# A load, attention work of two batches and one batch's phi moved in a fused linear attention and feed-forward kernel

## Chip, cores, metric

One core of one Trainium2 chip. The metric is device time of one execution in microseconds (us), the median of several.

## The reference, cut

```python
def phi(x):
    return np.where(x > 0, x, np.exp(x) - 1.0) + 1.0
# q, k, v: 8 batches, 8 heads, 576 positions, 64 per head
kv  = np.einsum('bhsd,bhse->bhde', phi(k), v)
z   = np.sum(phi(k), axis=2)
num = np.einsum('bhsd,bhde->bhse', phi(q), kv)
den = np.einsum('bhsd,bhd->bhs', phi(q), z)[..., None] + 1e-06
x   = (num / den)            # as 4608 tokens x 512
h   = x @ w_in               # 512 x 2048
out = (h - np.tanh(h)) @ w_out   # 2048 x 512
```

## The kernel before

The tokens go through the feed-forward part in nine chunks of 512. In a chunk, layer 1 makes 16 tiles of 128 hidden features (four matmuls each), a tanh on ScalarE (ACT) and a subtraction on VectorE (DVE) for two tiles at a time; layer 2 then has 16 slots of four matmuls. The attention of the next batches is sprinkled between: `s1[n]` is done behind tile n of layer 1, `s2[n]` behind slot n of layer 2.

```python
dense = Banks([0, 1, 2, 3, 4, 5])     # PSUM banks, in turn, for layers 1 and 2 from chunk 1 on
attn = Banks([6, 7])                  # for the attention of batches 2 and up

def l1act2(fi, h, gT):                # two tiles: their banks come free with the subtraction
    th = mpool.tile([128, 2, 512], F32, name="th")
    nc.scalar.activation(th, h, AF.Tanh)
    nc.vector.tensor_sub(gT[:, fi:fi + 2, :], h, th)                    # L373

# one half of phi of q or k: exp on ACT, then two instructions on DVE
(lambda: nc.scalar.activation(e, x, AF.Exp),                            # L134
 lambda: nc.vector.tensor_scalar(r, x, 0.0, 1.0, ALU.max, ALU.add),     # L135
 lambda: nc.vector.tensor_tensor(y, e, r, ALU.min))                     # L136

def a_spread(b):                      # 1/den to DRAM (ds) and back, spread over partitions (rdb)
    ds = dram.tile([H, 4, J * 16], F32, name="ds")
    for t in range(4):
        nc.sync.dma_start(out=ds[:, t, :], in_=rden_t[b][32 * t:32 * t + H, :])    # L305
    rdb = rpool.tile([128, NP, 4, J, 16], F32, name="rdb")
    for hh in range(2):
        nc.sync.dma_start(out=rdb[64 * hh:64 * hh + 64]...,                        # L308
                          in_=ds[4 * hh:4 * hh + 4]....partition_broadcast(64))
...
# the loads of a later batch wait until the transposing DMA of the next batch's q has landed
s1[0].append(lambda: (gate(qT_t[n1]), load_k(n2), load_q(n2), load_v(n2)))
...
elif n1 < B:                          # chunk 1: kv and den of batch 2 behind tiles 8 and 10
    s1[8 if c == 1 else 5].append(lambda: a_kv_cols(n1, attn))
    s1[10 if c == 1 else 8].append(lambda: (a_den(n1, attn), a_spread(n1)))
    for p in range(NP + 1):           # num, scaled by rdb, behind slots 12, 13, 14, 15, 15
        s2[min(12 + p, 15) if c == 1 else 9 + p].append(lambda p=p: a_num(n1, p))
```

`a_kv_cols` needs `vp`, a copy of v that VectorE makes (`a_vp`, L189). `a_num` puts a matmul (L317) into bank 6 or 7, which comes free when VectorE has multiplied by rdb (L328).

## Time and profile before

| | us |
|---|---|
| time, median of the 5 runs that go with the changed kernel's | 293.38 (293.09 to 293.61) |
| span of the profiled execution | 291.8 |
| TensorE busy | 285.5 (98%) |
| chunk 1: layer 1 starts, layer 2 starts | 50.24, 65.93 |
| chunk 2 starts | 80.72 |

The place where the change acts is 38 to 82 us. These are rows of TensorE's timeline there: start, length, engine and line, operation, result and operands, shapes, count, and in brackets the idle time just before and what ended it. A matmul's length is modelled and reaches into the next one's start: 512 columns show 0.379 us but start 0.216 apart, so read starts, and add 0.16 us to a bracketed idle time that follows such a matmul.

```profile
38.87 1.66 PE L177 MATMUL ps_all<-v,kp 64*128 64x192 bf16 x36 [0.22 <-DMA v<-in_v_dram]
...
50.24 8.07 PE L366 MATMUL ps_all<-xT,w_in_sb 128*128 128x512 bf16 x36
58.24 1.24 PE L199 MATMUL ps_all<-vp,kp 64*128 64x136 bf16 x36
...
65.93 11.39 PE L387 MATMUL ps_all<-w_out_sb,gT 128*128 128x512 bf16 x52
77.16 0.38 PE L317 MATMUL ps_all<-qT,kz 128*128 128x512 bf16 x1
...
79.31 0.38 PE L317 MATMUL ps_all<-qT,kz 128*128 128x512 bf16 x1
...
80.72 5.34 PE L366 MATMUL ps_all<-xT,w_in_sb 128*128 128x512 bf16 x24
```

The first row is kv of batch 1, with its wait for v. From 50.24 on come nine tiles (36 matmuls), kv of batch 2, the other seven tiles with den in between, layer 2, and the num matmuls between its last slots. None of these rows has a bracket; from the starts, TensorE loses some 0.2 us up to kv of batch 2 (36 x 0.216 from 50.24 is 58.0), 0.1 of it the gap that other narrow groups have ahead of them too, and nothing to speak of after.

### The profile page before, as it was taken

The numbers are of one execution on the slowest core, as the hardware profiler recorded it, in microseconds if no ns is written. First come the engines' busy times: TensorE is split into PE (matmuls) and PEld (weight loads), VectorE is DVE, ScalarE is ACT, GpSimd is POOL, SyncE is SP. The second block draws the span as 40 slices with busy tenths as digits, with TensorE's granted clock in tenths as the row PEclk, the third lists the DMA queues.
The fourth block names the chain that finished last, engine by engine and source line by source line (L and its number), as shares of the span: only waits on it lengthen the run. The fifth ranks groups of instructions, "written<-read, shape, count | busy, mean of one in ns | idle before, by whom it ended". The sixth has DMA issues, their size and how long they took to land.

```text
span 291.8 us, 4505 instructions
## 1 busy us (share of the span) xinstructions
PE 285.5 (98%) x1803; PEld 134.5 (46%) x1803; DVE 175.1 (60%) x266; ACT 139.7 (48%) x168; POOL 33.7 (12%) x56
## 2 busy tenths in 40 slices
PE   8999999999999999999999999999999999999994
PEld 3544464454454444444454444444544444444443
DVE  4759958987468674776478637865581457106600
ACT  4938548846354733465345534751551155126411
POOL 8674030110030003000300030000000000000000
PEclk9999999999999999999999999999999999999999
DMA  7999999997999768965895579666117310130032
GB/s 105 193 202 212 208 206 215 194 183 149 249 158 161 175 128 137 197 146 121 136 223 123 123 139 197 146 138 139 30 38 165 73 36 0 43 83 19 0 74 72
DMA packets 39093, 38.94 MB, mean 133 GB/s; under 512 B 16352, under 2 KB 33824, under 8 KB 38304
## 3 DMA queue, kind: packets, MB, share of 16 engines
q0 software_dynamic: 17568, 18.35, 39.0%
q1 hardware_dynamic: 21344, 20.17, 30.9%
q8 instruction: 14, 0.23, 0.3%
q10 hardware_dynamic: 160, 0.13, 0.1%
q14 instruction: 7, 0.06, 0.1%
HBM read 43.91 MB, written 9.55 MB: 183 GB/s over the span
## 4 chain that ended last, share of the span: by engine, by line
PE 85%; DMA 11%; POOL 2%; issue 1%; DVE 0%; POOLq 0%
PE ps_all L387 39%; PE ps_all L366 38%; DMA v<-in_v_dram 6%; DMA w_in_sb<-in_moe_w_in_dram 3%; PE ps_all L199 2%; DMA kraw<-in_k_dram 2%; PE ps_all L317 2%; PE ps_all L618 1%; PE ps_all L276 1%; POOL v L419 1%; PE ps_all L177 1%; POOL qraw L90 0%; PE ps_all L320 0%; POOL qraw L93 0%; POOL w_out_sb L115 0%
## 5 line engine op out<-in xcount | busy, mean ns | idle before, releaser
L366 PE MATMUL ps_all<-xT,w_in_sb 128*128 128x512 bf16 x574 | 127.6, 379 | 0.0
L387 PE MATMUL ps_all<-w_out_sb,gT 128*128 128x512 bf16 x560 | 127.5, 379 | 0.0
L373 DVE TENSOR_TENSOR gT<-ps_all,th 128x1024 bf16<-128x1024 f32 x64 | 77.9, 1218 | 59.2 <-ACT th L372 59.2
L372 ACT ACTIVATE th<-ps_all 128x1024 f32<-128x1024 f32 x64 | 65.6, 1025 | 57.1 <-PE ps_all L366 46.5
L366 PEld LDWEIGHTS <-w_in_sb 128*128 128x128 bf16 x574 | 55.0, 98 | 66.1 <-issue 0.3
L387 PEld LDWEIGHTS <-gT 128*128 128x128 bf16 x560 | 54.2, 98 | 64.2
L396 ACT COPY osb<-ps_all 128x512 f32<-128x512 f32 (+1 forms) x36 | 20.9, 583 | 71.8 <-PE ps_all L387 52.6
L328 DVE TENSOR_TENSOR xT<-ps_all,rdb 128x512 bf16<-128x512 f32 x24 | 16.5, 691 | 13.7 <-PE ps_all L317 11.2
L134 ACT ACTIVATE e<-qraw 128x1152 bf16<-128x1152 bf16 x16 | 18.5, 1160 | 8.2 <-DMA qraw<-in_q_dram 8.2
L134 ACT ACTIVATE e<-kraw 128x1152 bf16<-128x1152 bf16 x15 | 17.5, 1164 | 0.3 <-DMA kraw<-in_k_dram 0.3
L136 DVE TENSOR_TENSOR qp<-e,r 128x1152 bf16<-128x1152 bf16 x16 | 12.1, 758 | 8.0 <-ACT e L134 7.2
L136 DVE TENSOR_TENSOR kp<-e,r 128x1152 bf16<-128x1152 bf16 x15 | 11.4, 759 | 7.9 <-ACT e L134 6.9
L383 POOL COPY g<-qT 1x1 bf16<-1x1 bf16 x5 | 0.9, 178 | 119.2 <-DMA qT<-qp 119.2
L378 DVE TENSOR_TENSOR gT<-ps_all,th 128x512 bf16<-128x512 f32 x16 | 10.3, 686 | 2.4 <-ACT th L377 1.7
L377 ACT ACTIVATE th<-ps_all 128x512 f32<-128x512 f32 x16 | 9.2, 598 | 4.4 <-PE ps_all L366 3.2
L447 PE MATMUL ps_all<-zero 128*128 128x512 bf16 x29 | 9.2, 480 | 1.2 <-DVE zero L405 1.2
L317 PE MATMUL ps_all<-qT,kz 128*128 128x512 bf16 x28 | 10.1, 379 | 0.0
L135 DVE TENSOR_SCALAR r<-qraw 128x1152 bf16<-128x1152 bf16 x16 | 7.3, 454 | 2.1 <-DMA qraw<-in_q_dram 2.1
L199 PEld LDWEIGHTS <-kp 64*128 64x128 bf16 x216 | 6.4, 94 | 2.5 <-issue 2.1
L285 DVE RECIPROCAL rden<-den 128x144 f32<-128x144 f32 x7 | 7.4, 1053 | 0.2
L199 PE MATMUL ps_all<-vp,kp 64*128 64x136 bf16 x216 | 7.4, 220 | 0.0
L394 DVE COPY osb<-ps_all 128x128 f32<-128x128 f32 x1 | 0.3, 292 | 11.6 <-PE ps_all L618 11.6
(85 smaller groups left out, 123.6 us busy)
## 6 DMA issues: line engine op xcount, KB each, us to landing
out_dram<-osb SPq DMA_DIRECT2D x70, 128.0 KB
rdb<-ds SPq DMA_DIRECT2D x12, 576.0 KB
kraw<-in_k_dram POOLq DMA_DIRECT2D x7, 576.0 KB, 7.1
qraw<-in_q_dram POOLq DMA_DIRECT2D x7, 576.0 KB, 9.1
v<-in_v_dram POOLq DMA_DIRECT2D x7, 576.0 KB, 11.6
w_in_sb<-in_moe_w_in_dram POOLq DMA_DIRECT2D x6, 256.0 KB, 8.7
w_out_sb<-in_moe_w_out_dram POOLq DMA_DIRECT2D x3, 512.0 KB, 14.7
qraw<-in_q_dram POOLq DMA_DIRECT2D x2, 288.0 KB, 4.4
```

The source lines that it names most:

```text
L134: return (lambda: nc.scalar.activation(e, x, AF.Exp), lambda: nc.vector.tensor_scalar(r, x, 0.0, 1.0, ALU.max, ALU.add), lambda: nc.vector ...
L136: lambda: nc.vector.tensor_tensor(y, e, r, ALU.min))
L199: nc.tensor.matmul(ps[hg][:, i, :], kp[r, i, j].rearrange("p h d -> p (h d)"), vp[r, i, j, :], start=(j == 0), stop=(j == J - 1))
L317: nc.tensor.matmul(ps, kz[:, p // 2, p % 2, 0:128], qT[:, p % 2, 0:8, p // 2, :], start=True, stop=True)
L328: nc.vector.tensor_mul(xT[:, p, S * b:S * b + 512].rearrange("p (j t c) -> p j t c", j=8, t=4), ps.rearrange("p j (t c) -> p j t c", t=4), ...
L366: nc.tensor.matmul(h, w_in_sb[:, 2 * (p % 2) + p // 2, fi * 128:(fi + 1) * 128], xT[:, p, c * 512:(c + 1) * 512], start=(n == 0), stop=(n ...
L372: nc.scalar.activation(th, h, AF.Tanh)
L373: nc.vector.tensor_sub(gT[:, fi:fi + 2, :], h, th)
L377: nc.scalar.activation(th, h, AF.Tanh)
L378: nc.vector.tensor_sub(gT[:, fi, :], h, th)
L387: nc.tensor.matmul(o, gT[:, fi, i * 128:(i + 1) * 128], w_out_sb[:, fi, :], start=(fi == 0), stop=(fi == NF - 1))
L396: nc.scalar.copy(osb[:, f0:f1], o[:, f0:f1])
```

## The change

The intent, as the diff reads: TensorE stood idle for 0.4 us in chunk 0, waiting for v of batch 1. So kv of batch 1 goes two slots later (behind slot 9, with den and num behind slot 10), and half of a quarter of w_out, which slots 8 and 9, now ahead of kv, need, is loaded ahead of v. With attention of batch 1 later, phi of batch 2 moves later too: VectorE's part of k between the subtractions of chunk 1, v's copy, kv and den of batch 2 behind it. Chunk 1's first two tiles take pairs 0 and 1 of xT first.

```diff
-    load_v(1)
     for n in range(2):
+        if n == 1:
+            load_v(1)
         nc.gpsimd.dma_start(out=w_out_sb[:, 8 + 2 * n:10 + 2 * n, :], ...)
@@ chunk 0, behind slots of layer 2
-            s2[7].append(lambda: (a_qT_pe(1, 0, side), a_kv(1, side), a_qT_pe(1, 1, side)))
-            s2[8].append(lambda: b0_scale_rest(side))
-            s2[9].append(lambda: (a_den(1, side), num1(), a_split(1)))
-            s2[11].append(lambda: spread1(0))
+            s2[7].append(lambda: a_qT_pe(1, 0, side))
+            s2[8].append(lambda: a_qT_pe(1, 1, side))
+            s2[9].append(lambda: a_kv(1, side))
+            s2[10].append(lambda: (b0_scale_rest(side), a_den(1, side), num1(), a_split(1)))
+            s2[12].append(lambda: spread1(0))
-            s2[11].append(lambda: (exp2(qs, q_t, qp_t, "qp", 0), rest2(qs[0])))
+            s2[11].append(lambda: exp2(qs, q_t, qp_t, "qp", 0))
             s2[12].append(lambda: exp2(qs, q_t, qp_t, "qp", 1))
-            s2[13].append(lambda: (spread1(1), exp2(ks, k_t, kp_t, "kp", 0), rest2(qs[1]), a_qT_dma(2)))
-            s2[14].append(lambda: rest2(ks[0]))
+            s2[14].append(lambda: (spread1(1), exp2(ks, k_t, kp_t, "kp", 0), rest2(qs[0])))
+            s2[15].append(lambda: (rest2(qs[1]), a_qT_dma(2)))
@@ chunk 1, behind tiles of layer 1
-            s1[8 if c == 1 else 5].append(lambda: a_kv_cols(n1, attn))
-            s1[10 if c == 1 else 8].append(lambda: (a_den(n1, attn), a_spread(n1)))
+            s1[10 if c == 1 else 5].append(lambda: a_kv_cols(n1, attn))
+            s1[12 if c == 1 else 8].append(lambda: (a_den(n1, attn), a_spread(n1)))
-            s1[1].append(lambda: a_kphi(2, 1))
-            s1[3].append(lambda: (a_vp(2, 0), a_vp(2, 1)))
+            s1[1].append(lambda: (exp2(ks, k_t, kp_t, "kp", 1), rest2(ks[0])))
+            s1[3].append(lambda: rest2(ks[1]))
+            s1[5].append(lambda: (a_vp(2, 0), a_vp(2, 1)))
-            if c == 2 and fi == 1:            # the first two tiles: pairs 0, 1 of both, then 2, 3
+            if c in (1, 2) and fi == 1:
```

(`exp2` starts a half's exp on ScalarE, `rest2` does its two instructions on VectorE. The matching `elif` of the last hunk is left out.)

More of the change, by code (lines that the diff above doesn't have):

```diff
@@ L595 @@
                             l1mm(c, f, o, p, p)
-            elif c != 2 or fi > 1:
+            elif c not in (1, 2) or fi > 1:
                 for p in range(NP):
```

## The prediction

> **What bounds the kernel now.** I read the page's busy shares first, then the chain that ended last in order of time, then the timeline of each engine between 28 and 82 us, where the diff acts.
>
> ```profile
> PE 285.5 (98%) x1803; PEld 134.5 (46%) x1803; DVE 175.1 (60%) x266; ACT 139.7 (48%) x168; POOL 33.7 (12%) x56
> ```
>
> TensorE (PE) is the bound. The diff removes no matmul and adds none (the order of instructions shows 3546 PE rows in both), so the only thing to win or lose is PE idle time after the start-up. A dense matmul takes 13.81 us / 64 = 0.216 us, from the chain's row of 64 in the last chunk. With that I laid the chunks' work out and looked for holes.
>
> ```profile
> 22.32 16.50 DMA v<-in_v_dram
> 38.83 0.04 issue
> 38.87 1.66 PE ps_all L177 x36
> ...
> 232.66 13.81 PE ps_all L366 x64
> ```
>
> These are rows of the chain. The load of v of batch 1 is issued at 22.32 and lands at 38.83; kv of batch 1 (L177) starts right then. Before it, nine transposes (0.51 us by their spacing) start at 37.98 and end at 38.49: a hole of 0.38 us. About 0.10 us of such a hole stays anyway, as it does ahead of other narrow groups (12 dense from 87.24 end at 89.83, yet L276 starts at 89.94). So 0.28 us is won if v is no longer waited for. The other holes: 0.10 us ahead of L354 at 46.20 (waits for w on VectorE) and some 0.13 us near 52.1 (9th matmul of chunk 1, waits for the eviction of bank 2). From 53 us on I find none. All that can be won is therefore about 0.5 us of 293.31, under 0.2%: a speed-up of 2% is out of reach.
>
> **What the Trainium skill says.** (1) "TensorE: Matmul & The Clock Gate", section "Wait — 56ns, not 53.3ns?", gives 215.7 ns start to start for 512 columns at the full clock. The trace agrees (215.8), with a granted clock of 1.0 throughout. (2) "PSUM — Partial Sum Buffer", section "Engine vs sequencer instructions", says that the queues of ScalarE and VectorE are strict FIFO. The trace agrees: every row below runs in program order, also where a later one had its inputs. This is what the case turns on: what is put ahead of a subtraction on VectorE delays it. (3) "DMA: Bandwidth & Descriptors", section "Queues, rings and completion order", says that each DMA engine takes descriptors of a ring in order and goes round-robin between rings by packets. The trace fits: the queue of POOL has a backlog of 16 us at v, and swapping two loads in it swaps their places.
>
> **The change part by part.**
>
> Part 1, half a quarter of w_out ahead of v. In 30 to 38.9 us the DMA moves 207 GB/s (table by stretch; it counts the bf16 bytes). 256 KB is 1.27 us, v (576 KB) is 2.85 us. So w_out rows 8:10 land at 38.83 - 2.85 + 1.27 = 37.2 and v at 40.1; the sum, and with it the landing of everything behind, is unchanged.
>
> Part 2, slots of layer 2 in chunk 0. PE after the change: transposes from 37.98 to 38.49, slot 8 (4 x 0.216) to 39.35, its w_out being there 1.3 us earlier; transposes to 39.87, slot 9 to 40.73, kv at 40.83 with v 0.7 us early. kv takes 1.59 to 42.42, slot 10 to 43.29, batch 0's remainder 0.11, den at 43.5. den needs kz: VectorE starts it 0.1 after kv and takes 0.89, 43.4, so it just fits. The rest keeps its old distances (the 0.10 us for w included). Chunk 1 begins at 49.95 rather than 50.24: 0.28 us won here.
>
> Part 3, chunk 1's first two tiles take pairs 0, 1 first. Pairs 2 and 3 of xT come at about 50.0 and 50.75 and are needed at 51.0: fine. But tile 1 now writes bank 1 after two matmuls, at 50.38, and its eviction on ScalarE, which hangs behind the landing of q of batch 2, ends at 50.51: 0.19 us lost. The eviction of bank 2 now comes ahead of an exponential: the 0.13 us is won.
>
> Part 4, phi of k between activations. ScalarE does the same work up to the first tanh of chunk 1 (exponentials of q, q, k and four evictions, from 47.34, gated by the landing of q), so the first tanh stays at 52.41 and the first subtraction on VectorE at 53.50. VectorE before:
>
> ```profile
> 53.50 1.23 DVE L373 TENSOR_TENSOR gT<-ps_all,th 128x1024 bf16<-128x1024 f32 x1 [0.41 <-ACT th L372]
> 54.64 0.45 DVE L135 TENSOR_SCALAR r<-kraw 128x1152 bf16<-128x1152 bf16 x1
> 55.19 0.76 DVE L136 TENSOR_TENSOR kp<-e,r 128x1152 bf16<-128x1152 bf16 x1
> 55.87 1.22 DVE L373 TENSOR_TENSOR gT<-ps_all,th 128x1024 bf16<-128x1024 f32 x1
> 57.00 0.82 DVE L189 COPY vp<-v 128x1152 bf16<-128x1152 bf16 x2
> 57.74 2.35 DVE L373 TENSOR_TENSOR gT<-ps_all,th 128x1024 bf16<-128x1024 f32 x2
> ```
>
> It is full here. A subtraction costs 1.14 us start to start, a phi pair (r and min) 1.23, the two vp copies 0.74. The subtraction of tiles 4 and 5 starts at 57.74 and frees banks 4 and 5 at 58.9. Tile 10 takes bank 4 (six banks in turn); it starts at about 60.3 since kv of batch 2 (1.17 + 0.10) sits after tile 8. So it has a slack of 1.3 us.
>
> After: 53.50 subtraction, 54.64 phi of k half 0, 55.87 subtraction, 57.00 phi of k half 1, 58.23 subtraction of 4 and 5, which ends at 59.45. Only then vp. And kv has gone from behind tile 8 to behind tile 10, so PE comes to tile 10 at 49.95 + 0.19 + 8.63 = 58.8. It must wait to 59.5: 0.7 us (0.1 of it at tile 8, for bank 2, free at 57.1). So the time won in chunk 0 is lost again, and more: tile 10 to 60.4, kv to 61.6, tiles 11 to 15 and den to 66.4, where layer 2 of chunk 1 began at 65.93. Net so far **+0.5 us**.
>
> Part 5, what follows from den being two tiles later. VectorE: subtractions 60.11 and 61.25, kz 62.39, the subtraction of tiles 10, 11 at 63.75, then den and the reciprocal, ended at 66.3 instead of 64.06. SyncE sends it out and back:
>
> ```profile
> 51.93 3.23 SPq L153 DMA_TRANSPOSE qT<-qp  x1
> ...
> 64.09 1.28 SPq L305 DMA_DIRECT2D ds<-rden  x4
> 69.44 1.12 SPq L308 DMA_DIRECT2D rdb<-ds  x2
> ...
> 77.87 1.48 DVE L328 TENSOR_TENSOR xT<-ps_all,rdb 128x512 bf16<-128x512 f32 x2 [2.39 <-DMA rdb<-ds]
> ```
>
> rdb landed at 77.87 and was waited for. The third num matmul at 79.31 needs bank 6, freed by that first scaling (0.69): a slack of 0.7 us. ds goes out 2.2 us later now. Also the transposing DMA stands behind all eight output DMAs on SyncE: it starts at about 54.3 rather than 51.93, lands 2.4 us later, and the loads of batch 3, gated by it (56.88), move with it, so ds meets the same crowd. If the whole 2.2 us comes through, rdb lands at 80.1, bank 6 is free at 80.8, PE is there at 79.8: **1.0 us** of waiting. If DMA catches up half, 0. I take 0.8.
>
> Sum: 293.31 + 0.5 + 0.8 = 294.6. After chunk 2 PE has no hole to give it back.
>
> **The rivals.** A: the intent comes true, 0.3 to 0.5 us won, 292.9. For it: the hole at 38.5 is real, and v has 0.7 us to spare. Against it: VectorE's arithmetic of part 4, in which only durations from the trace stand. B: only the wait at tile 10 appears and rdb is in time, because the way out and back (8.4 us from L308 to the scaling) was stretched by the loads of batch 3 and may shrink when it meets fewer: 293.8. C: both waits in full, or rdb later still since the loads move 2.4 us, or a wait on w_out in slot 8 (if the loads don't follow the order of issue): 295 to 295.6. D: v still late for kv in slot 9, which would only move the wait, and is covered by the later wait at tile 10.
>
> **Range and chances.** A 15%, B 25%, the sum 45%, C 15%. Point 294.6, range 293.0 to 295.6. The runs before spread 0.5 us. 2% is 5.9 us, far outside of every rival: within 2% 0.98, faster 0.01, slower 0.01.
>
> **What would show it.** Right: kv (L177) at 40.7 to 40.9 without a DMA wait; layer 1 of chunk 1 starting near 49.95; the first subtraction (L373) near 53.5 and the third near 58.2; PE idle 0.5 to 0.8 us ahead of tile 10, released by L373; layer 2 of chunk 1 beginning near 66.4; the reciprocal ending near 66.3, the first scaling (L328) near 80, and an idle PE ahead of the third L317. From there on all is shifted alike. Wrong: the first subtraction earlier than 53 (ScalarE not gated by q), kv elsewhere, the scaling at 78.5 or sooner, or a chunk 1 no longer than before: then A or B.

## The result, and the profile after

| | before | after |
|---|---|---|
| time, median of 5 runs | 293.38 | 294.58 (294.35 to 294.77) |
| span of the profiled execution | 291.8 | 293.0 |
| layer 1 of chunk 1 starts | 50.24 | 50.01 |
| layer 2 of chunk 1 starts | 65.93 | 66.25 |
| ds sent, rdb sent back, rdb in use | 64.09, 69.44, 77.87 | 66.14, 71.35, 79.78 |
| chunk 2 starts | 80.72 | 81.93 |

The ratio is 1.0041 (95% interval 1.0026 to 1.0055). Ratios here are the mean time of one kernel's runs over that of the other's of the same rounds, so not quite the ratio of the medians quoted. The change costs 1.2 us, in a place of 44 us: chunk 2 starts 1.21 us later, and the span is 1.2 us longer.

TensorE's timeline after, for the rows shown of before:

```profile
40.87 1.66 PE L177 MATMUL ps_all<-v,kp 64*128 64x192 bf16 x36
...
50.01 8.90 PE L366 MATMUL ps_all<-xT,w_in_sb 128*128 128x512 bf16 x40
59.32 1.02 PE L366 MATMUL ps_all<-xT,w_in_sb 128*128 128x512 bf16 x4 [0.41 <-DVE gT L373]
60.28 1.24 PE L199 MATMUL ps_all<-vp,kp 64*128 64x136 bf16 x36
...
66.25 11.39 PE L387 MATMUL ps_all<-w_out_sb,gT 128*128 128x512 bf16 x52
77.47 0.38 PE L317 MATMUL ps_all<-qT,kz 128*128 128x512 bf16 x1
...
80.53 0.38 PE L317 MATMUL ps_all<-qT,kz 128*128 128x512 bf16 x1 [0.74 <-DVE xT L328]
...
81.93 5.34 PE L366 MATMUL ps_all<-xT,w_in_sb 128*128 128x512 bf16 x24
```

kv of batch 1 (L177) has no bracket any more: v is there. Layer 1 of chunk 1 starts 0.23 us sooner. Then two waits are new. Tile 10 (the row of 4 at 59.32) waits for a subtraction of VectorE: 40 matmuls from 50.01 would be through at 58.64, so 0.68 us are lost by then, most of it here (0.41, and the 0.16 of the modelled length). The third num matmul at 80.53 waits for the multiplication by rdb: the slot before it ends at 78.77 + 0.86 = 79.63, so 0.90 us. VectorE's rows behind the first wait:

```profile
53.46 1.22 DVE L373 TENSOR_TENSOR gT<-ps_all,th 128x1024 bf16<-128x1024 f32 x1 [0.31 <-ACT th L372]
54.60 0.45 DVE L135 TENSOR_SCALAR r<-kraw 128x1152 bf16<-128x1152 bf16 x1
55.08 0.76 DVE L136 TENSOR_TENSOR kp<-e,r 128x1152 bf16<-128x1152 bf16 x1
55.76 1.22 DVE L373 TENSOR_TENSOR gT<-ps_all,th 128x1024 bf16<-128x1024 f32 x1
56.89 0.45 DVE L135 TENSOR_SCALAR r<-kraw 128x1152 bf16<-128x1152 bf16 x1
57.38 0.76 DVE L136 TENSOR_TENSOR kp<-e,r 128x1152 bf16<-128x1152 bf16 x1
58.05 1.22 DVE L373 TENSOR_TENSOR gT<-ps_all,th 128x1024 bf16<-128x1024 f32 x1
59.19 0.82 DVE L189 COPY vp<-v 128x1152 bf16<-128x1152 bf16 x2
```

The third subtraction ends at 59.27, and tile 10, which needs its bank, starts at 59.32. Behind the second wait, rows of SyncE's and VectorE's timelines:

```profile
54.29 2.90 SPq L153 DMA_TRANSPOSE qT<-qp  x1
66.14 1.29 SPq L305 DMA_DIRECT2D ds<-rden  x4
71.35 1.12 SPq L308 DMA_DIRECT2D rdb<-ds  x2
...
79.78 1.89 DVE L328 TENSOR_TENSOR xT<-ps_all,rdb 128x512 bf16<-128x512 f32 x3 [3.99 <-DMA rdb<-ds]
```

ds is sent 2.05 us later than before, and rdb comes 1.91 us later: only 0.14 us of the delay is made up on the way.

### The profile page after: what moved, and what is told of

Read it like the earlier page. It is cut to its first block, busy times and chain, and to the rows that moved or that the text cites. A ratio compares the mean times of both kernels' runs of the same rounds, so it can differ in the third digit from the quotient of the medians. Undisturbed runs are those within 1.5% of the kernel's fastest.

```text
span 293.0 us, 4508 instructions
## 1 busy us (share of the span) xinstructions
PE 285.2 (97%) x1803; PEld 134.4 (46%) x1803; DVE 174.7 (60%) x266; ACT 139.7 (48%) x168; POOL 33.9 (12%) x56
## 4 chain that ended last, share of the span: by engine, by line
PE 69%; DMA 20%; ACT 3%; DVE 3%; issue 1%; SPq 1%; POOL 1%; DVEq 0%; POOLq 0%; ACTq 0%
PE ps_all L366 35%; PE ps_all L387 30%; DMA qraw<-in_q_dram 8%; DMA w_in_sb<-in_moe_w_in_dram 3%; DMA rdb<-ds 3%; DMA out_dram<-osb 2%; PE ps_all L199 2%; DMA kraw<-in_k_dram 2%; PE ps_all L317 2%; DMA ds<-rden 1%; ACT e L134 1%; ACT osb L396 1%; DVE gT L373 1%; PE ps_all L276 1%; SPq L401 0%
## 5 line engine op out<-in xcount | busy, mean ns | idle before, releaser
L317 PE MATMUL ps_all<-qT,kz 128*128 128x512 bf16 x28 | 10.1, 379 | 0.7 <-DVE xT L328 0.7
L448 PE MATMUL ps_all<-zero 128*128 128x512 bf16 x29 | 8.5, 453 | 1.2 <-DVE zero L405 1.2
L199 PEld LDWEIGHTS <-kp 64*128 64x128 bf16 x216 | 6.4, 94 | 2.5 <-issue 2.1
L199 PE MATMUL ps_all<-vp,kp 64*128 64x136 bf16 x216 | 7.4, 220 | 0.0
```

The source lines that it names most:

```text
L199: nc.tensor.matmul(ps[hg][:, i, :], kp[r, i, j].rearrange("p h d -> p (h d)"), vp[r, i, j, :], start=(j == 0), stop=(j == J - 1))
L317: nc.tensor.matmul(ps, kz[:, p // 2, p % 2, 0:128], qT[:, p % 2, 0:8, p // 2, :], start=True, stop=True)
```

## The experiments

All times below are of 5 or 6 timed runs of the experiment; the kernel before had 8 to 11 runs beside them, its medians 293.35 to 293.56. All gave the right result unless said otherwise. They ran on three chips, so each is compared with the kernel before of its own rounds. In single profiled executions the start-up differs: the first transposes of batch 1, up to which TensorE's list is the same in all kernels, came between 37.77 and 38.47. So absolute times of different kernels can differ by some 0.7 us for that reason alone; where tenths matter, count from that row (37.98 before, 38.04 after).

### Only the chunk 0 part

```diff
 from the changed kernel:
-  s2[12]: exp2(qs 1)              s2[14]: spread1(1), exp2(ks 0), rest2(qs[0])   s2[15]: rest2(qs[1]), a_qT_dma(2)
+  s2[12]: exp2(qs 1), rest2(qs[0])  s2[14]: spread1(1), exp2(ks 0), rest2(qs[1]), a_qT_dma(2)  s2[15]: rest2(ks[0])
+  s1[1]: a_kphi(2, 1); s1[3]: a_vp twice; kv and den of batch 2 behind tiles 8 and 10, as before
```

> The change with its chunk 1 part undone: loads, slots of layer 2 in chunk 0 and the order of pairs as in the change, but phi of k half 1, the copies of v, kv and den of batch 2 at the tiles of the kernel before. My theory (chunk 0 wins about 0.25 us, VectorE's order and the later den of chunk 1 lose it): layer 1 of chunk 1 starts near 50.0, no wait at tile 10, reciprocal near 64.2, rdb near 78; up to 0.3 us lost at tiles 1 and 2 (bank 1, pair 3). 293.1 to 293.4 us, against 294.6 of the change and 293.4 of the kernel before. Rival (the new order of chunk 0 costs by itself, for instance by loads or the output DMAs): 294 or more.

Measured: 293.48 us, ratio 0.9998 (0.9986 to 1.001): same. In the profile layer 2 of chunk 1 starts at 65.65 (before: 65.93), rdb is in use at 77.62, no wait. Of these 0.28 us, 0.21 are start-up (first transposes at 37.77). Counted from the first transposes, chunk 1 starts 0.28 us sooner than in the kernel before (11.98 us behind them, not 12.26), and loses 0.20 of it again up to kv of batch 2 (0.32 us lost beyond the usual gap, not 0.12).

The win itself is not in every execution. Three runs further below (late den, late transpose, both) leave chunk 0 of the kernel before as it was up to kv of batch 1. In their profiles kv starts 0.60, 0.67 and 0.60 us behind the first transposes, where nine transposes and the usual gap take 0.6; only in the profile before it is 0.89. The hole that the change is after was thus 0.3 us in one of four executions and 0.1 or nothing in the others.

My upper bound was 293.4, missed by 0.1, within the spread. What follows: this part of the change does no harm; the loss needs the rest. (The later transpose belongs to chunk 0 too, and is taken back by a slot here. It is tried by itself below.)

### Scaling without rdb

```diff
-                rdb[:, p, :, 0:8, :]...
+                (fake[:, :, 0:8, :] if b == 2 else rdb[:, p, :, 0:8, :])...    # fake: a tile of ones
```

> The change, but the scaling of batch 2 multiplies with a tile of ones instead of rdb (result wrong on purpose; rdb is still sent and lands unread). My theory (the last 0.7 to 0.9 us of the loss are the wait for rdb): no idle PE ahead of the third L317 in chunk 1, layer 2 of chunk 1 begins at 66.2 to 66.3 as in the change; 293.7 to 293.8 us. Rival (rdb only takes the blame, chunk 1's end is late anyway, by VectorE): 294.4 to 294.6.

Measured: 293.50 us, ratio 1.000 (0.9988 to 1.0012); the result is wrong, as meant. The third num matmul (L318 in this kernel) starts at 79.36 without a wait. With this one wait gone the whole loss is gone, 1.1 us rather than the 0.8 to 0.9 expected: in this execution layer 2 of chunk 1 begins at 65.98, hardly later than before (65.93). Up to kv only 0.27 us are lost in it, not 0.67 as in the change's profile, so the win in chunk 0 and the wait at tile 10 just cancel.

### The second half of k behind the third subtraction

```diff
-            s1[3].append(lambda: rest2(ks[1]))
-            s1[5].append(lambda: (a_vp(2, 0), a_vp(2, 1)))
+            s1[5].append(lambda: (rest2(ks[1]), a_vp(2, 0), a_vp(2, 1)))
```

> The change, but the phi of k half 1 on VectorE stands behind the third subtraction instead of ahead of it. My theory: the third subtraction starts near 56.9, no wait at tile 10, kv waits some 0.3 us for the copies of v, layer 2 of chunk 1 begins some 0.3 us earlier (65.9 to 66.0). But the reciprocal, and with it rdb's landing near 79.8, hardly move, so the time won is given back at the third L317, whose wait grows from 0.74 to about 1.0 us: 294.4 to 294.6. Rival (the two waits add): 294.1 to 294.2.

Measured: 294.64 us, as expected. TensorE's timeline:

```profile
59.91 1.24 PE L199 MATMUL ps_all<-vp,kp 64*128 64x136 bf16 x36
...
80.49 0.38 PE L317 MATMUL ps_all<-qT,kz 128*128 128x512 bf16 x1 [0.88 <-DVE xT L328]
```

The wait at tile 10 is gone, and the 0.3 us expected ahead of kv are not seen (44 matmuls from 50.32 and the usual gap of 0.10 make 59.9); layer 2 of chunk 1 starts at 66.07. But the third L317 starts at 80.49 as in the change (80.53), its wait grown from 0.74 to 0.88. rdb sets an absolute time, and whatever is won ahead of it on TensorE is given back there.

### The transposing DMA one slot earlier

```diff
-  s2[14]: ..., rest2(qs[0])              s2[15]: rest2(qs[1]), a_qT_dma(2)
+  s2[14]: ..., rest2(qs[0]), rest2(qs[1]), a_qT_dma(2)
```

> The change, but the transposing DMA of batch 2 is issued one slot earlier on SyncE, ahead of the last two output DMAs of chunk 0 (VectorE's order unchanged). My theory (ds lands when the loads of batch 3 are through, and these are gated by the transpose): transpose near 53.2 instead of 54.29, loads of batch 3 from 58.5 instead of 59.6, ds landed and rdb issued near 70.4 instead of 71.35, rdb near 78.8: the wait at the third L317 gone or under 0.2; 293.8 to 294.0 us. Rival (the landing of ds follows the reciprocal alone): rdb issued at 71.3 as in the change, 294.5 to 294.6.

Measured: 294.64 us (293.60 to 294.87); my theory's expectation missed. The transpose ran at 53.41 and the loads of batch 3 were issued 0.98 us sooner (58.62), but ds, sent at 65.93, let rdb go at 71.08, so 5.15 us later (in the change 5.21). Loads that came a little sooner were not enough: they still ran on for 3.5 us after ds was sent. Two of the six runs were at 293.60 and 294.07, the other four at 294.56 to 294.87: so this version may stand at an edge, which one profile, of one of the four, can't show.

### Only the later den

```diff
 from the kernel before:
-            s1[8 if c == 1 else 5]...a_kv_cols    s1[10 if c == 1 else 8]...a_den, a_spread
+            s1[10 if c == 1 else 5]...a_kv_cols   s1[12 if c == 1 else 8]...a_den, a_spread
```

> The kernel before with one thing of the change alone: kv of batch 2 behind tile 10 instead of tile 8, den behind tile 12 instead of tile 10. My theory now (the later den alone makes nearly the whole loss, through rdb): no more than 0.1 us of waiting at tile 10 (the third subtraction ends at 58.9, PE comes at 59.0), reciprocal ended near 65.8 instead of 64.06, rdb landed near 79.5, a wait of 0.8 to 1.0 us ahead of the third L317: 294.2 to 294.5 us. Rival (phi of k between the activations is what costs): 293.4 to 293.6.

Measured: 293.71 us, ratio 1.0005 (0.9991 to 1.0019). My expectation of 294.2 to 294.5 missed, and the row that says why is SyncE's:

```profile
65.51 1.29 SPq L305 DMA_DIRECT2D ds<-rden  x4
69.88 1.12 SPq L308 DMA_DIRECT2D rdb<-ds  x2
```

ds goes out 1.42 us later than before (64.09), but rdb follows after 4.37 us, not after 5.35 as before. rdb is in use at 78.53, and about 0.3 us are lost at the third L317 (79.28, where the slot before ended at 79.00). So the later den alone is nearly harmless.

### phi moved, kv and den where they were

```diff
 from the changed kernel:
-            s1[10 if c == 1 else 5]...a_kv_cols   s1[12 if c == 1 else 8]...a_den, a_spread
+            s1[8 if c == 1 else 5]...a_kv_cols    s1[10 if c == 1 else 8]...a_den, a_spread
```

> The change with kv and den of batch 2 put back behind tiles 8 and 10, phi of k still between the activations. My theory: kv must wait some 1.9 us for the copies of v, which now end near 60.0 on VectorE, so layer 2 of chunk 1 begins near 67.6, 1.7 us later than before; rdb comes in time for that: 294.9 to 295.3 us, slower than the change. It would show that the later kv is forced by the new order of phi. Rival (the earlier den saves rdb, and kv waits little): under 294.3.

Measured: 295.02 us, ratio 1.0053 (1.0040 to 1.0065), as expected. TensorE's row of kv of batch 2:

```profile
59.72 1.24 PE L199 MATMUL ps_all<-vp,kp 64*128 64x136 bf16 x36 [1.35 <-DVE vp L189]
```

With phi of k between the subtractions, v's copies end near 60 on VectorE, so kv behind tile 8 stands still for 1.35 us (1.5 with the modelled length). The later kv and den are not a second idea in the change; the first forces them.

### Only the order of loads

```diff
 from the kernel before: only the first hunk of the change (w_out rows 8:10 ahead of v of batch 1)
```

> The kernel before with the half quarter of w_out ahead of v of batch 1 and nothing else. My theory (the loads of POOL land in order of issue at 207 GB/s): v lands 1.27 us later, near 40.1, kv (L177) waits for it and starts near 40.15 instead of 38.87, and since that hole is PE's, chunk 1 starts 1.2 us later: 294.4 to 294.7 us. Rival (v's landing is not set by what is ahead of it in the queue): 293.4.

Measured: 294.44 us, ratio 1.0037 (1.0025 to 1.0050), as expected:

```profile
39.88 1.66 PE L177 MATMUL ps_all<-v,kp 64*128 64x192 bf16 x36 [1.11 <-DMA v<-in_v_dram]
```

v comes 1.0 us later than in the kernel before (38.87), near the 1.27 us worked out from 256 KB at 207 GB/s.

### v of batch 3 loaded after the reciprocal of batch 2

```diff
-            s1[0].append(lambda: (gate(qT_t[n1]), load_k(n2), load_q(n2), load_v(n2)))
+            s1[0].append(lambda: (gate(qT_t[n1]), load_k(n2), load_q(n2), c != 1 and load_v(n2)))
+            if c == 1:
+                s1[13].append(lambda: (gate_f(rden_t[2]), load_v(3)))   # copies one element of rden first
```

> The change, but the load of v of batch 3 waits for the reciprocal of batch 2 (a copy of one element on POOL), so ds does not meet it. The order of the loads of batch 3 ahead of ds is the point that the run with the earlier transpose left open. If ds stands behind the loads in the DMA engines: the loads of k and q end near 67.5, ds lands at 68.5 to 69.5 instead of 71.35, rdb (now beside the load of v) near 78 to 79, the wait at the third L317 under 0.3: 293.6 to 294.0 us. If the way of ds takes some 5.2 us whatever is in flight: rdb issued at 71.2 to 71.4, and 294.6 us or more.

Measured: 293.83 us (293.53 to 294.57), ratio 1.0014 (1.0002 to 1.0027), some 70% of the loss won back. ds sent at 66.11, rdb sent at 70.16: 4.05 us instead of 5.21, though not the 2.4 to 3.4 expected. rdb in use at 78.63, no wait at the third L317. So what is in flight on the DMA engines does stretch the way of ds.

### Only the later transpose

```diff
 from the kernel before:
-  s2[13]: ..., rest2(qs[1]), a_qT_dma(2)
+  s2[13]: ..., rest2(qs[1])             s2[15]: a_qT_dma(2)      # behind all eight output DMAs on SyncE
```

> The kernel before with one thing of the change alone: the transposing DMA of batch 2 behind all eight output DMAs of chunk 0 on SyncE. The reciprocal stays at 64.06. Theory 1 (late loads alone make ds late): transpose near 54.3, loads of batch 3 from 59.6, their end near 70.5, ds lands and rdb is issued 0.9 us after it, near 71.3, rdb near 79.7, a wait near 1.1 us at the third L317: 294.4 to 294.6 us. Theory 2 (ds needs both, a late reciprocal and late loads): rdb issued by 70 and landed by 78.4, no wait above 0.1: 293.4 to 293.6 us.

Measured: 293.55 us, ratio 1.0001 (0.9987 to 1.0015): theory 2. The loads of batch 3 moved as in the change (issued at 59.61), but:

```profile
63.92 1.29 SPq L305 DMA_DIRECT2D ds<-rden  x4
69.58 1.12 SPq L308 DMA_DIRECT2D rdb<-ds  x2
```

5.66 us after an unmoved reciprocal. ds does not wait until the loads are through: the DMA still moved 209 GB/s from 69 to 70 us. It takes its 5 to 6 us among them, and no more.

### Only the slots

```diff
 from the run with the chunk 0 part alone: v of batch 1 ahead of all of w_out, as before
```

> The run with the chunk 0 part alone, but with the loads in the order of the kernel before (v ahead of all of w_out). My theory (the slots and the load order need each other): slot 8 wants w_out rows 8:10 near 38.4, which land near 40.1, so PE waits some 1.6 us there instead of for v; 294.6 to 295.0 us. Rival (the order of loads is of no matter once kv stands in slot 9): 293.3 to 293.6.

Measured: 295.15 us, ratio 1.0057 (1.0044 to 1.0070), somewhat above my 294.6 to 295.0:

```profile
40.21 1.02 PE L387 MATMUL ps_all<-w_out_sb,gT 128*128 128x512 bf16 x3 [1.50 <-DMA w_out_sb<-in_moe_w_out_dram]
```

(One of the four matmuls has no record.) The order of loads alone and the slots alone each cost 0.9 to 1.6 us; only together are they harmless.

### An attempt at a version that beats both

```diff
 from the run with the chunk 0 part alone:
+  s2[12]: r of q half 0   s2[13]: exp of q half 1   s2[14]: spread1(1), min of q half 0, rest2(qs[1]), a_qT_dma(2)
+  s2[15]: exp of k half 0, rest2(ks[0])
```

> A version that might beat both: the chunk 0 part of the change, chunk 1 as before, and on ScalarE the evictions of banks 1 and 3 ahead of the exponentials of q half 1 and of k half 0; on VectorE the scaling of pairs 2 and 3 ahead of the min of q half 0. Theory: the wait for bank 1 (some 0.2 us) and for pair 3 go, kv of batch 2 starts near 57.75 instead of 57.95, the copies of v being next to bind; 293.1 to 293.3 us against 293.5 of the kernel before. If it is 293.5 or more, the front's 0.2 us are within the spread of runs or are lost again later.

Measured: 293.87 us, ratio 1.0009 (0.9996 to 1.0022): no better, and whether it is worse the interval leaves open. TensorE's row in chunk 1:

```profile
57.70 1.02 PE L366 MATMUL ps_all<-xT,w_in_sb 128*128 128x512 bf16 x3 [0.28 <-DVE gT L373]
```

With the evictions of banks 1 and 3 sooner, no bank holds up tiles 0 to 7, but VectorE reaches the first subtraction at 54.06 and the second at 56.43, so tile 8 waits instead. VectorE has no room in this stretch; a wait taken away ahead of it comes back behind it.

### Both delays on the kernel before

```diff
 from the kernel before: the later den and the later transpose, nothing else
```

> The kernel before with both delays and nothing else of the change: den of batch 2 two tiles later (alone: 293.7) and the transpose behind all output DMAs (alone: 293.55). Theory (ds takes 5.2 to 5.6 us as long as the loads of batch 3 run on, and less only when they end within 3 us): ds sent near 65.5 as with the late den alone, but rdb issued near 70.8 to 71.0 instead of 69.9, the first scaling near 79.3, a wait of 0.9 to 1.1 us ahead of the third L317: 294.3 to 294.6 us, the whole loss of the change without its chunk 0 part and without phi moved. Rival (the two delays only add, 0.2 and 0): 293.7.

Measured: 294.60 us (294.50 to 295.18), ratio 1.0047 (1.0033 to 1.0061). SyncE's and TensorE's rows:

```profile
65.65 1.29 SPq L305 DMA_DIRECT2D ds<-rden  x4
71.00 1.12 SPq L308 DMA_DIRECT2D rdb<-ds  x2
...
80.32 0.38 PE L317 MATMUL ps_all<-qT,kz 128*128 128x512 bf16 x1 [1.01 <-DVE xT L328]
```

This is as much as the whole loss of the change, with nothing else of it. The two delays, one by one and together:

| | transpose as before | transpose behind all outputs |
|---|---|---|
| den behind tile 10 | 293.5 | 293.55 |
| den behind tile 12 | 293.71 | 294.60 |

Against the kernel before of the same rounds (293.53, 293.56 and 293.35), the late den alone costs 0.2 us, the late transpose alone 0, both together 1.25. The rows say how. A late den alone meets DMA engines that are nearly done with batch 3: in that run the DMA's throughput fell from 207 GB/s in 67 to 68 us to 66 in 68 to 69, 2.8 us after ds had been sent, and ds took 4.37. A late transpose moves the loads of batch 3 by 2 us, so that the late ds meets the same crowd and takes 5.35 again. The Trainium skill, "DMA: Bandwidth & Descriptors", section "Issuing engines are not separate DMA queues", says that DMAs issued by different engines run on the same 16 DMA engines and interleave; the runs agree: ds is issued by SyncE and the loads by POOL, and its way takes 4.05 to 5.66 us beside them, against 2.35 us in chunk 6 of the kernel before (sent at 214.14, rdb sent at 216.49), where no load is left.

Over all fourteen profiles the way of ds goes with the time for which the loads run on after it is sent (until the DMA's throughput falls under 100 GB/s): 2.2 to 2.9 us where they are through or end within 0.9 us, 3.69 where they run on for 2.1 us (chunk 2 of the run without rdb), 4.37 for 2.8 us (late den alone), 5.15 for 3.5 us (earlier transpose), and then no longer in proportion, 5.02 to 5.66 for 3.9 us and more. Only the run that held back v of batch 3 stands apart: k and q end 1.2 us after ds was sent, but v's load then begins beside it.

## Why the prediction was right, and where not

The time (294.58 for 294.6) and its two causes came as predicted; their shares did not.

- **Parts 1 and 2, loads and slots: right.** kv of batch 1 at 40.87 (40.83) without a wait; layer 1 of chunk 1 at 50.01 (49.95). Each half of the pair alone fails (294.44 and 295.15), through the two waits for DMA that part 1 reckons with; that the swap of loads swaps their places was only asserted there, and the run with the order of loads alone shows it. What the prediction could not see in its one profile is that the wait for v, and so the 0.28 us to be won, is missing in other executions.
- **Part 3: right, small.** No wait for xT in chunk 1 shows. The 0.19 us for bank 1 don't show in the change's profile: of the 0.68 us lost up to tile 10 all but about 0.1 are at tile 10. (The run with the chunk 0 part alone does lose 0.20 us more than before up to kv.)
- **Part 4, the wait for the third subtraction: right in kind, too large.** The first subtraction came at 53.46 (53.50) and the third at 58.05 (58.23). The term that was off is the phi pair: r and min took 1.16 us start to start (54.60 to 55.76, 56.89 to 58.05), not the 1.23 of the kernel before. The min now starts 0.48 us after r instead of 0.55; why, no run tests. Layer 2 of chunk 1 started 0.32 us later, not 0.5. The wait also changes with the execution: in three runs with the same chunk 1 (no rdb, earlier transpose, v after the reciprocal) 0.26 to 0.27 us are lost up to kv, not 0.67, because the first subtraction starts 3.05 us behind the beginning of chunk 1 there and 3.45 us in the change's profile.
- **Part 5, rdb: right, too small.** ds left 2.05 us later (2.2), the way back was no shorter, rdb came 1.91 us later, and TensorE lost 0.90 us by the timeline, 1.1 us by the run without rdb, where I took 0.8, a guess between 1.0 and 0 without a working. That the loads of batch 3 had to move with it was named there, and the last run shows that it was needed. The rival in which DMA catches up is what the later den alone does (293.71).
- **The sum: right, but its two terms are not two costs.** The second wait ends at a time set by DMA (VectorE's chain up to the reciprocal, then ds and rdb), so taking away the first changes nothing (294.64). The whole loss is that one date: the third num matmul starts at 80.53 instead of 79.31, so 1.22 us late, and in the prediction's terms at 79.8 + 0.8 = 80.6. That 0.5 was too large and 0.8 too small had to cancel, since what TensorE doesn't lose ahead of this date it waits for there. Luck was only the guessed 0.8, that is, how much of the delay DMA would make up.

Not settled: why the way of ds grows no further than 5 to 6 us however long the loads run on, and why two of six runs with the earlier transpose did without most of the loss.

## What to carry to other kernels

When the bound engine is busy 98% of the time, a change is worth what it does to the few dates that other engines set for it; list these dates with their slack (here 0.7 us for rdb, 1.3 us for the third subtraction) before moving anything. A wait that ends at a date set elsewhere swallows every win ahead of it. Two moves that cost 0 and 0.2 us alone can cost 1.25 together when one was the other's room, as here the early loads were the late den's; so try both alone and both together. And a hole of 0.3 us in one profile may not be there in the next: look for it in several before working on it.

## What the Trainium skill lacked or had wrong

- "DMA: Bandwidth & Descriptors" has a fixed cost of about 2 us for one DMA (section "Anatomy of one DMA — SWDGE (gpsimd) path") and the interleaving of queues, but no figure for a small DMA from SyncE beside a backlog of loads: from sending four pieces of 4.5 KB to sending rdb, which waits for them, it was 5.02 to 5.66 us where the loads ran on for 3.5 us or more, 4.37 us where they ended after 2.8 us, and 2.35 us where no load was left.
- "TensorE: Matmul & The Clock Gate", section "Back-to-back issue gap", gives about 131 ns per matmul of 512 columns and 81 ns of 128 for a stream of weight loads and matmuls, and calls 216 ns an over-count. Here such streams run at 216 ns (64 matmuls in 13.81 us) and 58 ns (nine transposes in 0.52 us), as the page's own section "Wait — 56ns, not 53.3ns?" has it. I found no figure there for the gap ahead of a group of narrow tiles behind dense ones: 0.10 us ahead of L276, L199 and L354 in the kernel before.
- "Perfetto Trace Analysis", section "Tensor Engine Instruction (MATMUL, LD_WEIGHTS)", says that a matmul's end is modelled, but not by how much idle time is then shown too short: 0.74 us were shown where the starts make it 0.90, since a matmul of 512 columns is drawn 0.379 us long.
